# An mLSTM and feed-forward kernel on one core: raw query and key stacks, split on chip, and a result's round trip on GpSimd's queue

## The chip, the core and the metric

The kernel runs on one core of a Trainium2 chip. The core has five engines with a queue of instructions each: TensorE (PE) multiplies matrices, VectorE (DVE) and ScalarE (ACT) work on vectors, GpSimd (POOL) does the same more slowly, and SyncE (SP) issues DMA transfers. ACT and POOL can issue DMAs too. Every queue is worked off in order; an instruction that waits for a semaphore holds up everything behind it on its engine. Data lie in HBM, in the on-chip memory with 128 partitions (SBUF) and in the accumulators behind PE (PSUM). The metric is the device time of one execution in microseconds (us).

## The reference

For each of 4 x 8 chains (batch, head) a recurrent memory runs over 768 tokens, with head size 40; its output goes through a feed-forward layer of width 2048.

```python
def _attn_ref(q, k, v, i_gate, f_gate, o_gate):          # q, k, v: (4, 8, 768, 40)
    for t in range(S):
        m_new = np.maximum(f_gate[:, :, t] + m, i_gate[:, :, t])
        f_stab = np.exp(f_gate[:, :, t] + m - m_new)
        i_stab = np.exp(i_gate[:, :, t] - m_new)
        m = m_new
        C = f_stab[:, :, None, None] * C + i_stab[:, :, None, None] * np.einsum('bhd,bhe->bhde', vt, kt)
        n = f_stab[:, :, None] * n + i_stab[:, :, None] * kt
        h_tilde = np.einsum('bhde,bhe->bhd', C, qt)
        denom = np.maximum(np.abs(np.einsum('bhd,bhd->bh', n, qt)[:, :, None]), 1.0)
        y[:, :, t] = h_tilde / denom / (1.0 + np.exp(-o_gate[:, :, t]))

def _moe_ref(x, w_in, w_out):                            # x: (3072, 320)
    h = x @ w_in
    return (np.maximum(h, 0.0) + np.log1p(np.exp(-np.abs(h)))) @ w_out
```

## The kernel before

**Tiles and steps.** The 3072 tokens are cut into 24 steps of 128 tokens (one batch, one chunk of 128), and three steps make one tile of 384 tokens for the feed-forward layer: 8 tiles of 3 steps. A step does the memory in chunk form: scores of keys with queries (`scores`, PE tile sp), decays by a scan (`decay`, pw from fb), the product with the old state (`inter_wide`, iq), the values (`values_wide`, yq), and the new state (`state`, cp; cn). The first six steps (tiles 0 and 1) are "plain" and the other 18 "wide".

**The feed-forward layer.** For each of 16 chunks f of the hidden width, `products` multiplies the tile's input X with w_in into hp (8 matmuls), ACT takes the softplus twice (`activation`: gh rounded, and hp in place), DVE takes the difference gl, and two chunks later PE does 9 matmuls into po. Every number stands as a rounded high part and a remainder, since a single pass of PE keeps fewer bits. A tile's first matmul needs X of all three of its steps.

**Stacks of three.** A wide step's sp and iq use 120 partitions: three groups of 40, which hold q as (high, high, low) and k as (high, low, high), so that one pass sums the three partial products. Before the change `prepare` loads q and k of a whole tile (120 partitions are the three steps' 40 each), ACT rounds them (hiq, hik), POOL takes the remainders in place (loq, lok), and `load` copies six pieces of 40 partitions a step into the stacks qst and kst by DMA. The old state's stack cs is made otherwise (`stack`): ACT multiplies the threefold state with a mask of rows, lowk, and rounds; POOL subtracts that from the state. On masked rows the remainder is left, on the others the rounded value.

**The round trip of a step's result.** A wide step's result has the heads in pairs on partitions; `values_wide` writes y to HBM (yd, two DMAs), and `read_wide` reads it back by features (yx, three DMAs) and the denominators spread (nw, one). All six are issued from ACT's queue. Then `finish_wide` and `end_wide` make X: nm, its reciprocal and a product with the output gate eg on DVE, the product with yx on DVE, a rounding on ACT (X) and a subtraction on DVE.

**Order.** All instructions are put in order by a list of due times: one tick is one matmul of `products`. Each step has a base tick, and the numbers W_... are offsets to it; `-1000 - n` means n ticks after the last part. So a queue's order follows from the numbers, and the scheduler keeps it (`in_order`). In the wide stages the steps are a third of a tile, some 91 ticks, apart.

```python
    (W_LOAD, W_FB, W_SCAN, W_CN, W_CS, W_VW, W_SP0, W_SP1, W_Y, W_CP, W_CD,
     W_IQ0, W_IQ1, W_VI, W_YQ, W_YD, W_RD, W_FIN) = (
        -48, -52, 4, 19, -6, 4, 6, 14, 17, 31, 47, 50, 62, 38, 68, 79, 107, 139,
    )
```

Of the kernel before, what the change touches and what calls it, by code (L numbers as in the profile page):

```python
# [16 lines left out]
L = 128  # L17
NG = 3
# [21 lines left out]
def mlstm_moe_kernel(  # L40
# [44 lines left out]
    )  # L85
    GB = 3
# [54 lines left out]
    def later_gates():  # L141

        w = S - L
        ig = p1.tile([NCHAIN, w], F32, tag="hiq", name="ig")
        fg = p1.tile([NCHAIN, w], F32, tag="hik", name="fg")
# [13 lines left out]
        d1 = p1.tile([NCHAIN, w], F32, tag="loq", name="d1")  # L159
# [86 lines left out]
    def weights_out(u):  # L246
# [19 lines left out]
    def prepare(t):  # L266

        yield 0
        parts[t] = []
        for nm, src in zip("qk", qk[t]):  # L270
            lo = p1.tile([D3, H, L], F32R, tag=f"lo{nm}", name=f"lo{nm}{t}")
            nc.sync.dma_start(lo.bitcast(F32), src)
            parts[t].append([lo])
        yield PRD
        for (lo,), nm in zip(parts[t], "qk"):
            hi = p1.tile([D3, H, L], F32R, tag=f"hi{nm}", name=f"hi{nm}{t}")
            nc.scalar.copy(hi, lo.bitcast(F32))
            parts[t]["qk".index(nm)] = hi, lo
            yield -1000 - 5
        for hi, lo in parts[t]:  # L280
            for h in range(0, H, 4):
                h2 = slice(h, h + 4)
                nc.gpsimd.tensor_tensor(lo[:, h2], lo[:, h2].bitcast(F32), hi[:, h2], op=ALU.subtract)
                yield -1000 - PSY

    PRD, PSY = 24, 10

    parts = {}
# [5 lines left out]
    park = dpool.tile([B, D, H, E2], F32, name="park")  # L294
# [95 lines left out]
    def decays(z):  # L390

        z.fbs = []
        h0 = z.b * H
        for i in range(2):
            if z.s < 2:
                fb = ps_h.tile([128, HG, L], F32, tag="hp", name=f"fb{z.n}_{i}")
                for j in range(HG):
                    h = h0 + i * HG + j
                    nc.tensor.matmul(
                        fb[:, j, :], ident[:, h : h + 1].broadcast_to([128, 128]), fg0, start=True, stop=True  # L400
                    )
            else:
                fb = p2.tile([128, HG, L], F32, tag="fb", name=f"fb{z.n}_{i}")
                nc.sync.dma_start(fb, fz_d[z.c, h0 + i * HG : h0 + (i + 1) * HG, :].partition_broadcast(128))
            z.fbs.append(fb)
# [136 lines left out]
    def values_wide(z):  # L542

        yq = ps_a.tile([PP + EP, HG, L], F32, tag="pa", name=f"yq{z.n}")
        for h in range(H):
            p, i = divmod(h, 2)
            e0, e1 = i * PP, PP + i * EP
            nc.tensor.matmul(  # L548
                yq[e0:e1, p, :], z.via[:, h * E : h * E + e1 - e0], z.pws[h // HG][:, h % HG, :], start=True, stop=True
# [8 lines left out]
        rows = z.yd.rearrange("(d p i) t -> i d p t", p=HG, i=2)  # L558
        for i in range(2):
            nc.scalar.dma_start(rows[i], z.y[i * PP : i * PP + EP])  # L560

    def read_wide(z):
        z.yx = stage.tile([128, 3, L], F32, tag="sg", bufs=3, name=f"yx{z.n}")
        nc.scalar.dma_start(z.yx[:, 0:2], z.yd[0:256].rearrange("(c p) t -> p c t", p=128))
        for i in range(2):
            nc.scalar.dma_start(z.yx[i * 64 : (i + 1) * 64, 2], z.yd[256:DM])
        z.nq = p1.tile([128, L], F32, tag="sig", name=f"nw{z.n}")
        nc.scalar.dma_start(z.nq, z.yd[DM : DM + H].partition_broadcast(128 // H))
# [34 lines left out]

    def first_tile():
# [39 lines left out]
        for z in zs:  # L644
            z.sig = og[:, z.g].rearrange("p (h d) -> p h d", d=D)
# [63 lines left out]
        for i in range(NG, NH):  # L709
            nc.sync.dma_start(sgp[i], og[:, i])  # L710
# [252 lines left out]
    with in_order():  # L963
# [59 lines left out]
```

## Time and profile before

| what | value |
|---|---|
| median of 3 runs | 542.46 us (539.95 to 544.23) |
| the profiled execution | 546.57 us |
| its span, first to last instruction | 544.8 us |
| mean granted TensorE clock | 0.931 |
| DMA moved | 80.63 MB, mean 148 GB/s |

The span is what the trace covers; the execution's time has 1.7 us around it. A line of instruction groups reads: line of the kernel, engine, operation, what it writes and reads, shapes, count, then busy us and mean ns of one, then idle time of the engine ahead of it and what ended that. In a timeline a row has its start, its length, the engine (a q behind it marks its queue, which issues a DMA), and in brackets the idle time ahead and its releaser. In the list of waits a row is: who waited, for whom, us in all, times, longest us. A row of one tile's instructions has shortest, median and longest in ns. PE's ends are modelled, and a DMA's row is the time of its issue, not of its landing.

The DMA engines by slice of a 40th of the span, in tenths of full use:

```profile
DMA  7746881755553764648563866476664763111001
```

### The profile page before, as it was taken

The page shows a single profiled execution, that of the slowest core. Times are in us where ns is not written, and L with a number is a line of the kernel's source. Part 1 is how long each engine was busy: PE and PEld are TensorE (multiplying, and loading weights), DVE is VectorE, ACT ScalarE, POOL GpSimd, SP SyncE. Part 2 cuts the span into 40 slices and gives each one's busy share as a digit, 9 for nine tenths or more (in the row PEclk, how much of TensorE's full clock was granted, in tenths as well). Part 3 has the DMA queues.
Part 4 walks back from the last instruction along what each step waited for, and adds up shares of the span by engine and source line. Part 5 has one row for each costly group of instructions (what it writes and reads, how often), then busy time and mean ns, then how long its engine had stood idle before and what let it go on. Part 6 is the DMA issues. An engine that isn't in the chain of part 4 may idle for free.

```text
span 544.8 us, 9179 instructions
## 1 busy us (share of the span) xinstructions
PE 484.1 (89%) x3368; PEld 458.1 (84%) x3368; DVE 328.3 (60%) x522; ACT 206.1 (38%) x409; POOL 178.2 (33%) x217
## 2 busy tenths in 40 slices
PE   7478779787989868999889989998899979999997
PEld 7467678677989858999889978997899979999997
DVE  7776976976747536754675647672675566544221
ACT  2427343336325233425243253434342443234332
POOL 4258787986506203232205203510223211100000
PEclk9859887886999987999989999999899979999999
DMA  7746881755553764648563866476664763111001
GB/s 199 218 147 191 237 232 55 214 173 164 159 158 108 204 184 129 169 130 223 170 177 98 207 195 188 109 201 186 168 169 126 198 186 102 34 36 37 1 1 36
DMA packets 65951, 80.63 MB, mean 148 GB/s; under 512 B 7842, under 2 KB 46930, under 8 KB 65906
## 3 DMA queue, kind: packets, MB, share of 16 engines
q1 hardware_dynamic: 44594, 67.85, 44.4%
q10 hardware_dynamic: 21312, 12.20, 8.2%
q8 instruction: 26, 0.43, 0.3%
q14 instruction: 19, 0.16, 0.1%
HBM read 52.41 MB, written 8.30 MB: 111 GB/s over the span
## 4 chain that ended last, share of the span: by engine, by line
PE 58%; DMA 18%; DVE 9%; ACT 5%; issue 4%; POOL 3%; SPq 1%; ACTq 1%; DVEq 0%; POOLq 0%
PE hp L928 25%; PE po L899 23%; DMA yd<-y 5%; PE sp L484 3%; DMA fb<-fz_d 2%; PE cp L461 2%; PE yq L548 2%; DMA yx<-yd 2%; DMA eg<-in_oT 2%; DMA qst<-hiq 2%; DVE pw L413 2%; PE yp L517 1%; PE iq L537 1%; DMA cn<-cn 1%; DMA kst<-in_qk 1%
## 5 line engine op out<-in xcount | busy, mean ns | idle before, releaser
L928 PE MATMUL hp<-X,wih 128*128 128x384 f32 x768 | 191.4, 355 | 15.1 <-ACT X L585 12.5
L928 PEld LDWEIGHTS hp<-X,wih 128*128 128x128 f32 x768 | 140.0, 198 | 19.4 <-ACT X L585 13.9
L805 ACT ACTIVATE gh<-hp 128x384 fp32r<-128x384 f32 x128 | 62.6, 489 | 217.0 <-PE hp L928 116.7
L810 DVE TENSOR_TENSOR gl<-hp,gh 128x384 fp32r<-128x384 f32 x112 | 61.9, 553 | 127.0 <-ACT hp L807 126.8
L899 PE MATMUL po<-wol,gh 128*128 128x320 f32 x384 | 84.0, 320 | 7.7 <-POOL wol L252 7.7
L899 PE MATMUL po<-woh,gh 128*128 128x320 f32 x384 | 85.4, 321 | 6.1 <-ACT gh L805 3.9
L899 PE MATMUL po<-woh,gl 128*128 128x320 f32 x384 | 85.9, 321 | 0.0
L301 POOL TENSOR_TENSOR cs<-cn,cs 120x336 fp32r<-120x336 f32 x15 | 20.5, 1366 | 175.8 <-ACT cs L300 147.4
L899 PEld LDWEIGHTS po<-woh,gh 128*128 128x128 f32 x384 | 67.4, 196 | 8.6 <-ACT gh L805 4.8
L899 PEld LDWEIGHTS po<-wol,gh 128*128 128x128 f32 x384 | 63.8, 194 | 9.6 <-POOL wol L252 8.4
L928 PE MATMUL hp<-X,wil 128*128 128x384 f32 x256 | 71.2, 356 | 0.0
L413 DVE TENSOR_TENSOR_SCAN pw<-fb,ident 128x512 f32<-128x512 f32 x48 | 64.4, 1383 | 9.3 <-DMA fb<-fz_d 7.7
L899 PEld LDWEIGHTS po<-woh,gl 128*128 128x128 f32 x384 | 64.2, 194 | 0.6 <-issue 0.4
L807 ACT ACTIVATE hp<-hp 128x384 f32<-128x384 f32 x112 | 54.6, 487 | 0.0
L928 PEld LDWEIGHTS hp<-X,wil 128*128 128x128 f32 x256 | 47.8, 198 | 1.2 <-issue 0.9
L540 DVE TENSOR_TENSOR y<-iq,y 41x512 f32<-41x512 f32 x36 | 24.5, 681 | 32.6 <-PE iq L537 32.4
L484 PEld LDWEIGHTS sp<-qst,kst 120*128 120x128 f32 (+2 forms) x240 | 34.8, 204 | 6.7 <-issue 3.1
L484 PE MATMUL sp<-qst,kst 120*128 120x128 f32 (+2 forms) x240 | 35.7, 284 | 4.9 <-DVE X L599 2.7
L486 DVE TENSOR_TENSOR pw<-sp,pw 128x512 f32<-128x512 f32 x48 | 32.0, 681 | 1.9 <-PE sp L484 1.8
L585 ACT CAST X<-eg 128x384 fp32r<-128x384 f32 x18 | 9.2, 514 | 54.1 <-DVE eg L583 54.1
L810 POOL TENSOR_TENSOR gl<-ab,gh 128x384 fp32r<-128x384 f32 x16 | 19.5, 1219 | 12.7 <-ACT ab L807 11.1
L548 PE MATMUL yq<-pw,vi 128*64 128x128 f32 (+1 forms) x288 | 19.6, 278 | 2.8 <-DVE y L540 2.8
(124 smaller groups left out, 543.1 us busy)
## 6 DMA issues: line engine op xcount, KB each, us to landing
fb<-fz_d SPq DMA_DIRECT2D x44, 256.0 KB
vt<-in_vko SPq DMA_DIRECT2D x23, 324.0 KB
qst<-hiq SPq DMA_DIRECT2D x36, 160.0 KB
kst<-hik SPq DMA_DIRECT2D x36, 160.0 KB
wo<-in_w_out SPq DMA_DIRECT2D x8, 640.0 KB
wr<-in_w_in SPq DMA_DIRECT2D x8, 512.0 KB
out<-ob ACTq DMA_DIRECT2D x24, 160.0 KB
eg<-in_oT SPq DMA_DIRECT2D x6, 576.0 KB
```

Source lines behind the costliest of these rows:

```text
L301: nc.gpsimd.tensor_tensor(z.cs, z.old, z.cs, op=ALU.subtract)
L413: nc.vector.tensor_tensor_scan(pw.rearrange(flat), fb.rearrange(flat), ident4.rearrange(flat), 0.0, ALU.mult, ALU.add)
L461: nc.tensor.matmul(z.cp[:, h, :], z.kt[:, h * D : (h + 1) * D], z.vw[:, h, :], start=True, stop=True)
L484: nc.tensor.matmul(sp[:, j, :], z.kst[:, h, :], z.qst[:, h, :], start=True, stop=True)
L486: nc.vector.tensor_tensor(z.pws[i], sp, z.pws[i], op=ALU.mult)
L540: nc.vector.tensor_tensor(y, iq, y, op=ALU.mult)
L548: nc.tensor.matmul(yq[e0:e1, p, :], z.via[:, h * E : h * E + e1 - e0], z.pws[h // HG][:, h % HG, :], start=True, stop=True)
L805: nc.scalar.activation(gh, hp, AF.Softplus)
L807: nc.scalar.activation(ab, hp, AF.Softplus)
L810: (nc.vector if t else nc.gpsimd).tensor_tensor(gl, ab, gh, op=ALU.subtract)
L899: nc.tensor.matmul(po[j], a[:, j * 128 : (j + 1) * 128], w[:, f, :], start=(f == 0 and left[j] == 2), stop=(last and left[j] == 0),)
L928: nc.tensor.matmul(hp, a, r, start=(i == 0), stop=(i == len(seq) - 1))
```

## The change

- **Raw stacks.** The host lays q and k out per step and three times over, as 120 partitions of both. `prepare` and its four tiles go. A wide step loads all 120 partitions by one DMA (`load_raw`, due at -80), and `split` makes the stack as `stack` does the state's: per q and k one multiplication with a mask on ACT (lowq is new: 1 on the last 40 rows), then four subtractions of half the heads on POOL. q and k share one tile, qk. raw has one buffer, qk two.
- **The round trip** (yd, yx, nw) is issued from POOL's queue. The heads are paired (0, 4), (1, 5) and so on instead of (0, 1), (2, 3), so that y's rows and the decays behind it (fc) are runs of 2 KB instead of 512 bytes.
- **Smaller parts.** The parked state is written threefold by one DMA and read by one. fb is one tile per step with two buffers, loaded ahead of vt. The output gates of the first six steps come by three DMAs instead of six, q and k of the first tile by one each step instead of two.

```diff
-    def prepare(t):
...
+    def load_raw(z):
+
+        z.raw = p1.tile([D3, 2, H, L], F32, tag="raw", name=f"raw{z.n}")
+        nc.sync.dma_start(z.raw, qk[z.s])
+
+    def split(z):
+
+        z.qk = p2.tile([D3, 2, H, L], F32R, tag="qk", name=f"qk{z.n}")
+        z.qst, z.kst = z.qk[:, 0], z.qk[:, 1]
+        for i, low in enumerate((lowq, lowk)):
+            nc.scalar.activation(z.qk[:, i], z.raw[:, i], AF.Copy, scale=low[:D3])
+            yield SPA
+        for h in range(0, H, HG):
+            h2 = slice(h, h + HG)
+            for i in range(2):
+                nc.gpsimd.tensor_tensor(z.qk[:, i, h2], z.raw[:, i, h2], z.qk[:, i, h2], op=ALU.subtract)
+                yield SPL
+
+    SPA, SPL = 5, 7
...
-            (qh, ql), (kh, kl) = parts[t]
-            z.qst = p2.tile([D3, H, L], F32R, tag="qst", name=f"qst{n}")
-            z.kst = p2.tile([D3, H, L], F32R, tag="kst", name=f"kst{n}")
-            for r, (a, e) in enumerate(((qh, kh), (qh, kl), (ql, kh))):
-                nc.sync.dma_start(z.qst[r * D : (r + 1) * D].bitcast(F32), a[gs].bitcast(F32))
-                nc.sync.dma_start(z.kst[r * D : (r + 1) * D].bitcast(F32), e[gs].bitcast(F32))
...
-                for r in range(3 if t >= PLAIN else 1):
-                    nc.sync.dma_start(z.old[r * D : (r + 1) * D], park[z.b])
+                m = 3 if t >= PLAIN else 1
+                nc.sync.dma_start(z.old[0 : m * D].rearrange("p h e -> p (h e)"), park[z.b, 0:m].rearrange("r d f -> (r d) f"))
...
-            h = 2 * p + i
+            h = HG * i + p
...
-        rows = z.yd.rearrange("(d p i) t -> i d p t", p=HG, i=2)
+        rows = z.yd.rearrange("(d i p) t -> i d p t", p=HG, i=2)
         for i in range(2):
-            nc.scalar.dma_start(rows[i], z.y[i * PP : i * PP + EP])
+            nc.gpsimd.dma_start(rows[i], z.y[i * PP : i * PP + EP])
...
-        nc.scalar.dma_start(z.yx[:, 0:2], z.yd[0:256].rearrange("(c p) t -> p c t", p=128))
+        nc.gpsimd.dma_start(z.yx[:, 0:2], z.yd[0:256].rearrange("(c p) t -> p c t", p=128))
         for i in range(2):
-            nc.scalar.dma_start(z.yx[i * 64 : (i + 1) * 64, 2], z.yd[256:DM])
+            nc.gpsimd.dma_start(z.yx[i * 64 : (i + 1) * 64, 2], z.yd[256:DM])
...
-        nc.scalar.dma_start(z.nq, z.yd[DM : DM + H].partition_broadcast(128 // H))
+        nc.gpsimd.dma_start(z.nq, z.yd[DM : DM + H].partition_broadcast(128 // H))
...
     def wide_step(z):
-        yield W_LOAD if z.g else -45
-        load(z)
+        yield W_RAW
+        load_raw(z)
         yield W_FB
         decays(z)
+        yield W_LOAD
+        load(z)
+        yield from rel(split(z))
...
-    qk = np.stack(steps).reshape(NT, NG, 2, H, L, D).transpose(0, 2, 1, 5, 3, 4)
+    qk = np.stack(steps).transpose(0, 4, 1, 2, 3)
+    qk = np.concatenate([qk] * 3, axis=1)
```

**What moves on ACT.** ACT's queue ahead of a tile start, in the stage that ends at 323.87 us (gh_11 to X; names end in the chunk or step number and a count). Before:

```order
L805 ACTIVATE gh_11_2523<-hp_11_2508 128x384
L807 ACTIVATE hp_11_2508<-hp_11_2508 128x384
L564 DMA yx_3_2528<-yd_3_2460 128x2x128
L566 DMA yx_3_2528<-yd_3_2460 64x128 x2
L568 DMA nw_3_2532<-yd_3_2460 128x1x128
L805 ACTIVATE gh_12_2568<-hp_12_2550 128x384
L807 ACTIVATE hp_12_2550<-hp_12_2550 128x384
L336 ACT_TABLE_LOAD
L337 ACTIVATE eg_2475<-eg_2475 128x1152
L338 ACT_TABLE_LOAD
L805 ACTIVATE gh_13_2612<-hp_13_2589 128x384
```

And now:

```order
L811 ACTIVATE gh_11_2469<-hp_11_2452 128x384
L813 ACTIVATE hp_11_2452<-hp_11_2452 128x384
L811 ACTIVATE gh_12_2514<-hp_12_2496 128x384
L813 ACTIVATE hp_12_2496<-hp_12_2496 128x384
L318 ACT_TABLE_LOAD
L319 ACTIVATE eg_2419<-eg_2419 128x1152
L320 ACT_TABLE_LOAD
L358 ACTIVATE qk_5_2544<-raw_5_2459,lowq 120x1024
L358 ACTIVATE qk_5_2544<-raw_5_2459,lowk 120x1024
L811 ACTIVATE gh_13_2552<-hp_13_2538 128x384
```

The reads of yd are gone from between gh_11 and gh_12, and the two casts of the next step's stack stand between the second table load and gh_13.

**What moves on POOL.** POOL's queue over one wide step, from vw of one step to cs of the next. Before, at a place where no remainders of a tile fall:

```order
L440 TENSOR_TENSOR vw_4_2497<-vt_4_2380,gw_4_2494 128x328
L449 MEMSET cn_4_2541 40x8
L452 TENSOR_TENSOR cn_4_2541<-cn_3_2315,flast 40x8x41
L422 MEMSET vi_4_2582 128x7
L425 TENSOR_TENSOR vi_4_2582<-vt_4_2380,gT 128x328
L301 TENSOR_TENSOR cs_5_2715<-cn_4_2541,cs_5_2715 120x336
```

And now:

```order
L437 TENSOR_TENSOR vw_4_2441<-vt_4_2316,gw_4_2438 128x328
L563 DMA yx_3_2474<-yd_3_2404 128x2x128
L565 DMA yx_3_2474<-yd_3_2404 64x128 x2
L567 DMA nw_3_2478<-yd_3_2404 128x1x128
L446 MEMSET cn_4_2487 40x8
L449 TENSOR_TENSOR cn_4_2487<-cn_3_2264,flast 40x8x41
L419 MEMSET vi_4_2528 128x7
L422 TENSOR_TENSOR vi_4_2528<-vt_4_2316,gT 128x328
L363 TENSOR_TENSOR qk_5_2544<-raw_5_2459,qk_5_2544 120x512 x4
L559 DMA yd_4_2630<-y_4_2484 48x512 x2
L283 TENSOR_TENSOR cs_5_2659<-cn_4_2487,cs_5_2659 120x336
```

The reads of the step before stand between vw and cn, and the four subtractions and the write of the next result between vi and cs.

More of the change, by code (lines that the diff above doesn't have):

```diff
@@ L85, in mlstm_moe_kernel @@
     )
+    lowq = cpool.tile([128, 1], F32, name="lowq")
+    nc.gpsimd.memset(lowq, 1.0)
+    nc.gpsimd.affine_select(
+        lowq, lowq, pattern=[[0, 1]], compare_op=ALU.is_ge, fill=0.0, base=-2 * D, channel_multiplier=1
+    )
     GB = 3
@@ L143, in later_gates @@
         w = S - L
-        ig = p1.tile([NCHAIN, w], F32, tag="hiq", name="ig")
-        fg = p1.tile([NCHAIN, w], F32, tag="hik", name="fg")
+        ig = p1.tile([NCHAIN, w], F32, tag="ig", name="ig")
+        fg = p1.tile([NCHAIN, w], F32, tag="fg", name="fg")
         nc.sync.dma_start(fg, gates[0, :, L:])
@@ L158, in later_gates @@
         yield GR[2]
-        d1 = p1.tile([NCHAIN, w], F32, tag="loq", name="d1")
+        d1 = p1.tile([NCHAIN, w], F32, tag="raw", name="d1")
         nc.gpsimd.memset(d1, 0.0)
@@ L264, in mlstm_moe_kernel @@
     OF = [0, 8]
-    def prepare(t):
[L268 to L288, printed above, removed]
     Xs = {}
@@ L293, in mlstm_moe_kernel @@
     sgp = dpool.tile([NH, 128, DM], F32, name="sgp")
-    park = dpool.tile([B, D, H, E2], F32, name="park")
+    park = dpool.tile([B, 3, D, H * E2], F32, name="park")
     def stack(z):
@@ L401, in decays @@
                     )
[L402 to L405, printed above, removed]
+                z.fbs.append(fb)
+        if z.s >= 2:
+            fb = p2.tile([128, H, L], F32, tag="fb", bufs=FB, name=f"fb{z.n}")
+            for i in range(0, H, HG):
+                nc.sync.dma_start(fb[:, i : i + HG], fz_d[z.c, h0 + i : h0 + i + HG].partition_broadcast(128))
+            z.fbs = [fb[:, 0:HG], fb[:, HG:H]]
+    FB = 2
     def decay(z):
@@ L475, in new_state @@
         else:
-            nc.sync.dma_start(park[z.b], cn[0:D])
+            one = cn[0:D].rearrange("p h e -> p (h e)")
+            nc.sync.dma_start(park[z.b].rearrange("r d f -> d r f"), one.unsqueeze(1).broadcast_to([D, 3, H * E2]))
         yield
@@ L544, in values_wide @@
         yq = ps_a.tile([PP + EP, HG, L], F32, tag="pa", name=f"yq{z.n}")
-        for h in range(H):
-            p, i = divmod(h, 2)
+        for k in range(H):
+            p, i = divmod(k, 2)
+            h = HG * i + p
             e0, e1 = i * PP, PP + i * EP
             nc.tensor.matmul(
-                yq[e0:e1, p, :], z.via[:, h * E : h * E + e1 - e0], z.pws[h // HG][:, h % HG, :], start=True, stop=True
+                yq[e0:e1, p, :], z.via[:, h * E : h * E + e1 - e0], z.pws[i][:, p, :], start=True, stop=True
             )
@@ L602, in new_x @@
         Xs[t] = p2.tile([128, 6, T], F32R, tag="X", name=f"X{t}")
+    room = p1.tile([128, 2, H, L], F32, tag="raw", name="room")
     def first_tile():
@@ L626, in output_gates @@
         def output_gates(i0, i1):
-            for i in range(i0, i1):
-                b, c = ORDER[i]
-                nc.sync.dma_start(og[:, i], vko[b, c * L : (c + 1) * L, H * E + DM :])
+            part = vko[:, :, H * E + DM :].rearrange("b (c p) f -> p b c f", p=L)
+            if i0 == 0:
+                nc.sync.dma_start(og[:, 0:3], part[:, 0:3, 0])
+            else:
+                nc.sync.dma_start(og[:, 3], part[:, 3, 0])
+                nc.sync.dma_start(og[:, 4:6], part[:, 0, 1:3])
             yield
@@ L708, in first_tile @@
             state_values(z)
-        for i in range(NG, NH):
-            nc.sync.dma_start(sgp[i], og[:, i])
+        nc.sync.dma_start(sgp[NG:NH].rearrange("i p f -> p i f"), og[:, NG:NH])
         return zs
@@ L1003 @@
     arrays = {
-        "qk": qk.reshape(NT, 2, D3, H, L),
+        "qk": qk,
         "vko": np.concatenate([tok(v1), tok(k), tok(o)], axis=-1),
```

25 lines of the change are left out of this document (10 added, 15 removed).

## Prediction

> **What bounds the kernel now.** I read the page first (busy shares), then the stages of the five tiles between the first and the last two, then the waits of all engines, then the timeline ahead of one tile start.
>
> ```profile
> span 544.8 us, 9179 instructions
> PE 484.1 (89%) x3368; PEld 458.1 (84%) x3368; DVE 328.3 (60%) x522; ACT 206.1 (38%) x409; POOL 178.2 (33%) x217
> ```
>
> TensorE (PE) is the bound: no other engine is busy for more than 60%. The profiled execution took 546.57 us, 1.7 more than its span. What a change of the attention part can win is therefore PE's idle time, and time in which PE runs at a lower clock. The stages, each from one tile's first product to the next tile's, show both (microseconds from start to end, length, then busy time of each engine, granted clock, DMA):
>
> ```profile
> 143.13:206.44 63.31, 52.76 (x386) 49.37 (x384) 35.95 (x59) 22.85 (x46) 15.80 (x19) 0.95 0.60 166
> 206.44:263.71 57.27, 56.09 (x416) 53.62 (x417) 35.86 (x61) 22.13 (x43) 15.35 (x22) 0.97 0.59 164
> 263.71:323.87 60.16, 55.83 (x401) 52.76 (x401) 36.16 (x61) 22.83 (x45) 14.69 (x19) 0.97 0.61 169
> 323.87:383.22 59.35, 54.02 (x401) 51.19 (x401) 35.49 (x61) 22.75 (x45) 13.87 (x19) 1.00 0.64 170
> 383.22:442.32 59.10, 56.15 (x416) 53.49 (x416) 36.74 (x63) 22.75 (x45) 15.32 (x22) 0.97 0.62 170
> sum 299.19, PE 274.86 PEld 260.43 DVE 180.22 ACT 113.31 POOL 75.02; mean PE 54.97 PEld 52.09 DVE 36.04 ACT 22.66 POOL 15.00
> ```
>
> In these 299.2 us PE is idle for 299.19 - 274.86 = 24.3. GpSimd (POOL, the fifth busy column) works 14 to 16 us of about 60 in a tile, so it has room. The fourth tile, at clock 1.00, is busy 54.02 us; the three with 0.97 are busy 56.09, 55.83 and 56.15, together 6.0 us more, for about the same work. Who PE waited for, and what stood in the way on ACT:
>
> ```profile
> ACT gh L805 <- DMA yx<-yd: 36.0, 8, 7.2
> ACT gh L805 <- DMA yd<-y: 17.3, 4, 9.0
> PE hp L928 <- ACT X L585: 12.5, 5, 3.1
> PE po L899 <- POOL wol L252: 7.7, 3, 3.4
> PE po L899 <- ACT gh L805: 3.9, 2, 3.7
> PE cp L461 <- POOL cn L449: 2.9, 2, 1.6
> PE yq L548 <- DVE y L540: 2.8, 2, 1.8
> PE po L899 <- ACT ob L948: 1.9, 1, 1.9
> ```
>
> Five tile starts wait for X, 12.5 us in all. The other waits in the same stages come to 3.9 + 2.9 + 2.8 + 1.9 = 11.5, and 12.5 + 11.5 = 24.0 is nearly all of the 24.3. The wait for wol is in tile 0. ACT itself sat 36.0 + 17.3 us behind the write and reads of yd. One tile start shows how the two belong together:
>
> ```profile
> 301.76 0.64 ACTq L560 DMA_DIRECT2D yd<-y  x1
> 304.49 0.56 ACTq L560 DMA_DIRECT2D yd<-y  x1
> 306.83 0.91 POOL L301 TENSOR_TENSOR cs<-cn,cs 120x336 fp32r<-120x336 f32 x1 [11.23 <-DVE pw L413]
> 310.94 0.38 ACTq L564 DMA_DIRECT2D yx<-yd  x1
> 313.21 0.62 ACTq L568 DMA_DIRECT2D nw<-yd  x1
> 313.93 0.49 ACT L805 ACTIVATE gh<-hp 128x384 fp32r<-128x384 f32 x1 [6.42 <-DMA yx<-yd]
> 314.82 1.28 ACT L336 ACT_TABLE_LOAD   x1
> 318.60 0.49 ACT L805 ACTIVATE gh<-hp 128x384 fp32r<-128x384 f32 x1
> 319.50 0.56 DVE L810 TENSOR_TENSOR gl<-hp,gh 128x384 fp32r<-128x384 f32 x1 [3.52 <-ACT hp L807]
> 320.81 0.29 DVE L572 SCALAR_TENSOR_TENSOR nm<-nw 128x128 f32<-128x128 f32 x1
> 323.30 0.51 ACT L585 CAST X<-eg 128x384 fp32r<-128x384 f32 x1 [3.04 <-DVE eg L583]
> 323.87 1.21 PE L928 MATMUL hp<-X,wih 128*128 128x384 f32 x5 [2.45 <-ACT X L585]
> ```
>
> ACT's queue is in order. The read yx has to wait until the write of yd has landed (304.49 to 310.94), and gh, which needs only PE, stands behind it: ACT is idle for 6.42 us. The sigmoid with its two table loads (314.82 to 318.60) then comes late, the next gh with it, DVE's gl waits for that (3.52), and behind gl in DVE's queue stands nm, the first step to X. X comes 2.45 us late. POOL idled 11.23 us in that same stretch.
>
> **The change, part by part.** First the write and reads of yd, six DMAs a step, which go from ACT's queue to POOL's. What they and the work added cost:
>
> ```profile
> L283 POOL TENSOR_TENSOR loq<-loq,hiq x12: 1269/1287/2242, 78.2 to 409.0; 120x512 fp32r<-120x512 f32 x12
> L277 ACT CAST hiq<-loq x6: 1043/1050/1055, 72.1 to 403.1; 120x1024 fp32r<-120x1024 f32 x6
> L301 POOL TENSOR_TENSOR cs<-cn,cs x15: 907/954/1917, 116.6 to 465.7; 120x336 fp32r<-120x336 f32 x15
> L425 POOL TENSOR_TENSOR vi<-vt,gT 128x328 f32<-128x328 f32 x23 | 18.0, 784 | 5.3 <-DMA vt<-in_vko 5.3
> L440 POOL TENSOR_TENSOR vw<-vt,gw 128x328 f32<-128x328 f32 x19 | 14.6, 768 | 15.0 <-DVE gw L434 7.8 <-PE hp L928 3.0 <-PE sp L484 1.7
> L452 POOL TENSOR_TENSOR cn<-cn,flast 40x328 f32<-40x328 f32 x13 | 11.8, 904 | 0.0
> L560 ACTq DMA_DIRECT2D yd<-y x36: 565/611/1497, 141.0 to 479.8; - x36
> L566 ACTq DMA_DIRECT2D yx<-yd x36: 482/607/1453, 148.9 to 484.3; - x36
> L564 ACTq DMA_DIRECT2D yx<-yd x18: 366/383/429, 148.5 to 483.3; - x18
> L568 ACTq DMA_DIRECT2D nw<-yd x18: 548/606/911, 150.2 to 485.0; - x18
> ```
>
> *ACT's side.* At the tile start shown ACT loses its 6.42 us wait, and gains the two casts of the next step, 2 x 1.05 = 2.1 us, behind the table loads and ahead of gh_13. Net 6.42 - 2.1 = 4.3 us earlier, against 2.45 that X was late and 3.1 at the worst. So the five waits for X should nearly go. I leave 0.5 us each: 12.5 - 2.5 = 10.0 won. The waits for gh (3.9) and ob (1.9) are ACT's own and go: 5.8. Those of yq for DVE y (2.8) come from gl ahead of y in DVE's queue; I count 2.0. The wait for cn (2.9) I leave, since POOL's DMAs now stand ahead of cn.
>
> *POOL's side.* No DMA of POOL stands in this trace. The nearest rows are the same DMAs on ACT: at the medians 2 x 0.611 + 0.383 + 2 x 0.607 + 0.606 = 3.4 us a step, at the longest 2 x 1.497 + 0.429 + 2 x 1.453 + 0.911 = 7.2. At the shortest they are 3.0; a price below that, or a gain on POOL, is excluded because POOL had no DMA to lose. I take 6.0, or 1.0 each, nearer to the long end, because POOL does like work slower than the others. The Trainium skill (DMA: Bandwidth & Descriptors, section Latency and other measured facts) gives a DMA from GpSimd about 1 us to its first byte and one from SP or ACT about 0.6. By that page the six would be about 6 us as well; no run here shows it.
>
> A step's other work on POOL: four splits 4 x 1.287 = 5.1 (per step, before it was per tile), cs 0.95, vw 0.77, vi 0.78, cn 0.90, together 8.5. With the DMAs 14.5, between 11.5 and 15.7. A step has a third of a tile, 59.35 / 3 = 19.8 us, or 18.8 when 3 us of waiting a tile are gone. It fits, with 4.3 to spare. Behind POOL's wait for the landing of yd stand cn, vi and the splits of the next step. Cn is then about 4 x 1.0 us later than before; DVE's addition to cn would wait 1 to 2 us, and gl behind it has a lead of about two chunks on PE. For these new waits on PE (sp for qk, cp for cn) I put +1.5, from 0 to 5.
>
> *Raw stacks, one load.* Per step SP issues one DMA of 120 x 8 KB = 983 KB from HBM in place of six copies of 164 KB within the chip (983 KB as well) and a third of two loads of 492 KB. That is 328 KB and about six issues less. It is hidden beside PE either way; if it is not, the cast on ACT waits for it (a rival below). The load of fb moves ahead of that of vt in SP's queue; that costs nothing while vt lands before vi and vw, which come after the scan of fb. If vt came late, POOL would wait at vw, and yx behind it. The casts grow from two per tile to six, 4 x 1.05 = 4.2 us of ACT's 22.7 busy in a tile: hidden, and already counted at the tile start.
>
> *Clock.* The three stages at 0.97 were busy 6.0 us longer than the one at 1.00 would have been; if the lower clock comes from PE's idle time, it goes with it. The trace does not tie the two together, so I count half, 3.0 (0 to 6.0). The Trainium skill (TensorE: Matmul & The Clock Gate, Part 1) has the clock drop after an idle window of about 3.4 us; by that page waits of 3.1 us are too short, the term would be 0 and the sum -14.3.
>
> *Tile 0.* POOL is nearly full there. The splits of the first two wide steps cost 8 x 1.287 = 10.3 where four (5.1) stood before; the four of the first step come later than the old ones did, ahead of wol. POOL's idle time stands at the end of tile 0:
>
> ```profile
> 131.65 1.01 POOL L810 TENSOR_TENSOR gl<-ab,gh 128x384 fp32r<-128x384 f32 x1 [3.92 <-ACT ab L807]
> 141.21 1.71 POOL L252 TENSOR_TENSOR wol<-sgo,woh 128x320 fp32r<-128x320 f32 x2 [1.52 <-ACT woh L249]
> ```
>
> There 3.92 + 1.52 us cover the second step's four; PE's wait for wol (7.7) grows by the rest. I put +2.5, between 0 and 5.1.
>
> *First loads.* Q, k and og of the first tile come by fewer issues; the DMA engines were full there, so -0.5 (from +1, as both memsets now precede the load, to -2). Park (one threefold write and one load in place of three), fb's second buffer and the new pairing of heads add nothing to PE, DVE or ACT; SP's queue, which computes nothing, covers them, and were it late, the scan would wait for fb.
>
> **Sum.** -10.0 - 5.8 - 2.0 + 1.5 - 3.0 + 2.5 - 0.5 = -17.3 us. Against the profiled execution's 546.57 that is 529.3. The median of the runs shown is 542.46, 4.1 below that execution, and the change is compared by medians: 542.46 - 17.3 = 525.2, rounded 525.
>
> **Rivals.** (1) *X stays late.* The write of yd now stands behind four splits on POOL, and yx behind vw. For it: yx still waits for a landing, which took 5.9 us (305.05 to 310.94) in the stretch shown. Against it: cs ran there at 306.83 and vw takes 0.77 behind it, so both were done well ahead of yx at 310.94. The terms for X and clock then fall away: -17.3 + 13.0 = -4.3, or 538.
>
> (2) *POOL becomes the bound*, which ends slower. POOL's step is 8.5 + 6d against 18.8, so it decides from d = 1.7 us on. At d = 2.0 a step needs 20.5, 1.7 more, and over some 17 intervals +29: 542.5 - 17.3 + 29 = 554. For it: POOL's own rows stretch beside DVE, 1.287 to 2.242. Against it: that is the longest of twelve, and even ACT's longest issues make 1.2 on average. The Trainium skill (SBUF — State Buffer, section SBUF: two separate sides) warns of such a case: GpSimd cannot write its descriptors while VectorE is in a two-port mode. By that page VectorE's copies within SBUF do this, and the wide steps have none of these; no run here shows it.
>
> (3) *The load of raw lands late.* There is one buffer, so it starts only when the last split has read it, some 6 us ahead of the cast. If the cast on ACT waits 3 us at each tile start, X is late again by about as much: -17.3 + 15 = -2, or 540.
>
> **Chances.** The forecast 0.70, rival 1 0.13, rival 2 0.12, rival 3 0.05. A measurement of this kernel tells 1% (5.4 us) from no change: faster is below 537.0, slower above 547.9. The forecast's case is faster, 0.70. Rivals 1 and 3 lie within 1%, but with a longer wait rival 3 ends slower, for which I take 0.02 of its 0.05: same 0.13 + 0.03 = 0.16, slower 0.12 + 0.02 = 0.14. The low end of the range takes all 24.3 us of idle time, 6.0 of clock and 2 of first loads, less 2.5 for tile 0: -29.8, or 513. The high end takes in rivals 1 and 3: 541. That leaves out rival 2 and the tails.
>
> **What would show it.** Right: ACT's waits for yd and yx are gone; PE's wait for X is under 3 us in all; the stages are 55 to 57 us long; POOL is busy (with its queue) 40 to 47 us a tile. Rival 1: PE waits for X behind POOL's yx. Rival 2: sp waits for qk, cp for cn, in every step. Rival 3: ACT's cast waits for raw. The forecast fails if POOL's DMAs take over 1.8 us each, or if tile 0 loses more than 5 us.

## The result, and the profile after

| | before | changed |
|---|---|---|
| median of 4 runs | 543.35 us (539.95 to 545.69) | 559.49 us (556.51 to 562.45) |
| ratio | 1 | 1.0302 (95% interval 1.0223 to 1.0381) |
| the profiled execution | 546.57 us | 556.51 us |
| its span | 544.8 us | 554.8 us |
| mean granted TensorE clock | 0.931 | 0.941 |

The changed kernel is 3% slower; the forecast was 525 us, 3% faster. The profiled execution of the kernel before lies above its four runs, that of the changed kernel is the fastest of its four, so their spans differ by 10.0 us where the medians differ by 16.

Section 1 of the page of the changed kernel gives each engine's busy time:

```profile
PE 483.8 (87%) x3368; PEld 455.5 (82%) x3368; DVE 377.0 (68%) x522; ACT 232.4 (42%) x433; POOL 299.5 (54%) x375
```

PE is as busy as before (484.1), so what was lost is waiting. DVE is 48.7 us busier (328.3 before) with the same 522 instructions: some of them have become longer. The tables of instruction groups say which, first one row of before, then rows of the changed kernel:

```profile
L572 DVE SCALAR_TENSOR_TENSOR nm<-nw 128x128 f32<-128x128 f32 x18 | 5.2, 288 | 0.3
...
L571 DVE SCALAR_TENSOR_TENSOR nm<-nw 128x128 f32<-128x128 f32 x18 | 51.6, 2865 | 2.9 <-DMA nw<-yd 2.7
L363 POOL TENSOR_TENSOR qk<-raw,qk 120x512 fp32r<-120x512 f32 x72 | 93.8, 1327 | 1.6 <-ACT qk L358 1.5
L563 POOL DMA_DIRECT2D yx<-yd x18 | 14.1, 782 | 65.7 <-DMA yd<-y 65.7
L559 POOL DMA_DIRECT2D yd<-y x36 | 19.4, 540 | 54.9 <-DVE y L552 54.9
L565 POOL DMA_DIRECT2D yx<-yd x36 | 18.9, 529 | 0.0
L567 POOL DMA_DIRECT2D nw<-yd x18 | 10.0, 554 | 0.0
```

The 18 nm took 5.2 us before (0.29 each) and take 51.6 now. That is 46.4 of the 48.7 us. The list of PE's waits has, beside those of the first tiles, these:

```profile
PE hp L934 <- ACT X L584: 10.0, 5, 3.0
PE cp L458 <- POOL vw L437: 7.6, 6, 1.5
PE iq L535 <- DVE cn L463: 5.9, 7, 1.5
PE yq L547 <- POOL vi L422: 5.4, 3, 2.5
```

X is nearly as late as before (12.5), and PE now waits for vw, cn and vi, all of which are POOL's or behind POOL. It never waits for the subtractions themselves: no wait of sp for POOL's qk is in the list. The timeline ahead of the tile start at 328.53, the one that answers to 323.87 before, shows why:

```profile
308.64 1.07 POOL L559 DMA_DIRECT2D yd<-y  x2 [3.37 <-DVE y L552]
310.27 1.06 POOL L283 TENSOR_TENSOR cs<-cn,cs 120x336 fp32r<-120x336 f32 x1 [0.56 <-ACT cs L282]
312.75 0.74 POOL L437 TENSOR_TENSOR vw<-vt,gw 128x328 f32<-128x328 f32 x1 [1.41 <-PE hp L934]
316.64 0.79 POOL L563 DMA_DIRECT2D yx<-yd  x1 [3.16 <-DMA yd<-y]
318.48 0.55 POOL L567 DMA_DIRECT2D nw<-yd  x1
319.83 0.75 POOL L422 TENSOR_TENSOR vi<-vt,gT 128x328 f32<-128x328 f32 x1
320.52 5.08 POOL L363 TENSOR_TENSOR qk<-raw,qk 120x512 fp32r<-120x512 f32 x4
322.65 3.11 DVE L571 SCALAR_TENSOR_TENSOR nm<-nw 128x128 f32<-128x128 f32 x1
325.79 0.95 DVE L572 RECIPROCAL nm<-nm 128x128 f32<-128x128 f32 x1
327.37 0.56 DVE L582 TENSOR_TENSOR eg<-yx,eg 128x384 f32<-128x384 f32 x1
327.85 0.68 DVE L552 TENSOR_TENSOR y<-yq,y 112x512 f32<-112x512 f32 x1
327.96 0.51 ACT L584 CAST X<-eg 128x384 fp32r<-128x384 f32 x1 [5.61 <-DVE eg L582]
328.98 1.07 POOL L559 DMA_DIRECT2D yd<-y  x2 [3.37 <-DVE y L552]
```

Two things can be read here. First, nm starts in the midst of POOL's four subtractions and ends 0.16 us after the last of them (325.60). Secondly, the rows close a loop. The next step's y stands behind nm in DVE's queue, and its write yd, issued at 328.98, stands behind the subtractions in POOL's. From yd to yd it is 8.0 us to the reads (issue and landing), 2.4 of reads, 1.5 of cn and vi, 5.1 of subtractions, 0.2 until nm has ended, and 3.2 over the reciprocal, the gate, the product and y to the next yd: 20.34 us. Three steps make 61.0 us, and the last three wide stages took 60.6, 61.7 and 62.7 us (from the tile starts at 267.92, 328.53, 390.21 and 452.88). The chain that ended last says the same: from 149 to 454 us it goes back and forth between the landing of yd and nm, but for stretches of PE of 11 to 14 us behind the tile starts at 208.51, 267.92 and 328.53.

```profile
309.20 6.69 DMA yd<-y
322.65 3.12 DVE nm L571
...
350.36 6.33 DMA yd<-y
363.52 3.04 DVE nm L571
...
391.23 6.99 DMA yd<-y
404.50 3.55 DVE nm L571
```

### The profile page after: what moved, and what is told of

Its sections match the earlier page's. It is cut to its first block, busy times and chain, and to the rows that moved or that the text cites. A ratio compares the mean times of both kernels' runs of the same rounds, so it can differ in the third digit from the quotient of the medians.

```text
span 554.8 us, 9099 instructions
## 1 busy us (share of the span) xinstructions
PE 483.8 (87%) x3368; PEld 455.5 (82%) x3368; DVE 377.0 (68%) x522; ACT 232.4 (42%) x433; POOL 299.5 (54%) x375
## 4 chain that ended last, share of the span: by engine, by line
PE 28%; DVE 25%; DMA 20%; POOL 14%; issue 9%; ACT 3%; SPq 1%; POOLq 0%; DVEq 0%; ACTq 0%
DMA yd<-y 16%; PE hp L934 12%; PE po L905 11%; DVE nm L571 8%; DVE y L538 2%; DVE nm L572 2%; POOL qk L363 2%; DVE gl L816 2%; POOL yx L563 2%; DVE pw L410 2%; DMA ig<-in_gates 2%; POOL cn L449 2%; DVE eg L574 1%; DVE eg L582 1%; DVE y L552 1%
## 5 line engine op out<-in xcount | busy, mean ns | idle before, releaser
L934 PE MATMUL hp<-X,wih 128*128 128x384 f32 x768 | 189.1, 351 | 13.0 <-ACT X L584 10.0
L363 POOL TENSOR_TENSOR qk<-raw,qk 120x512 fp32r<-120x512 f32 x72 | 93.8, 1327 | 1.6 <-ACT qk L358 1.5
L905 PE MATMUL po<-woh,gh 128*128 128x320 f32 x384 | 83.4, 317 | 0.0
L410 DVE TENSOR_TENSOR_SCAN pw<-fb,ident 128x512 f32<-128x512 f32 x48 | 72.6, 1553 | 1.3 <-PE fb L392 1.3
L813 ACT ACTIVATE hp<-hp 128x384 f32<-128x384 f32 x112 | 54.4, 486 | 0.0
L571 DVE SCALAR_TENSOR_TENSOR nm<-nw 128x128 f32<-128x128 f32 x18 | 51.6, 2865 | 2.9 <-DMA nw<-yd 2.7
L563 POOL DMA_DIRECT2D yx<-yd x18 | 14.1, 782 | 65.7 <-DMA yd<-y 65.7
L463 DVE TENSOR_TENSOR cn<-cn,cp 40x328 f32<-40x328 f32 x16 | 7.8, 488 | 61.0 <-POOL cn L449 56.4
L559 POOL DMA_DIRECT2D yd<-y x36 | 19.4, 540 | 54.9 <-DVE y L552 54.9
L482 PEld LDWEIGHTS sp<-qk 120*128 120x128 f32 (+2 forms) x224 | 34.1, 213 | 9.2 <-issue 4.2
L482 PE MATMUL sp<-qk 120*128 120x128 f32 (+2 forms) x224 | 35.4, 294 | 6.6 <-DVE X L598 2.8
```

Of the source, the lines that this page charges most:

```text
L363: nc.gpsimd.tensor_tensor(z.qk[:, i, h2], z.raw[:, i, h2], z.qk[:, i, h2], op=ALU.subtract)
L410: nc.vector.tensor_tensor_scan(pw.rearrange(flat), fb.rearrange(flat), ident4.rearrange(flat), 0.0, ALU.mult, ALU.add)
L482: nc.tensor.matmul(sp[:, j, :], z.kst[:, h, :], z.qst[:, h, :], start=True, stop=True)
L559: nc.gpsimd.dma_start(rows[i], z.y[i * PP : i * PP + EP])
L563: nc.gpsimd.dma_start(z.yx[:, 0:2], z.yd[0:256].rearrange("(c p) t -> p c t", p=128))
L571: nc.vector.scalar_tensor_tensor(nm, z.nq, -1.0, z.nq, op0=ALU.mult, op1=ALU.max)
```

## The experiments

Two theories were set against others. **Lock**: an instruction of DVE with both operands in SBUF, such as nm, is held up for as long as POOL runs subtractions. **Loop**: the closed chain above sets the pace, so that each microsecond on it costs some 17 us in all, until PE is the bound again. Their first rival was **queue**: POOL's wait for the landing of yd holds the kernel up, whatever else is done. Each ratio is to runs of the kernel before taken along with that kernel, whose medians were 541.76 to 544.48 us.

| kernel | median us | ratio to before (95% interval) | nm, mean us | PE's wait for X, us |
|---|---|---|---|---|
| changed | 559.49 | 1.0302 (1.0223 to 1.0381) | 2.87 | 10.0 |
| DMAs on POOL alone | 538.56 | 0.9927 (0.9892 to 0.9961) | 0.34 | 3.7 |
| raw stacks alone | 569.94 | 1.0478 (1.0398 to 1.0557) | 0.79 | 19.5 |
| reciprocal first | 545.54 | 1.0050 (1.0010 to 1.0090) | 1.97 (absolute value) | 6.5 |
| y ahead of nm | 542.62 | 0.9975 (0.9935 to 1.0015) | 0.68 | 11.2 |
| half the subtractions behind yd | 551.51 | 1.0129 (1.0072 to 1.0186) | 0.36 | 2.9 |
| all four ahead of the reads | 588.94 | 1.0843 (1.0777 to 1.0909) | 0.32 | 7.9 |
| two ahead, two behind the reads | 580.85 | 1.0745 (1.0665 to 1.0825) | 0.61 | 9.1 |
| no subtractions | 517.21 | 0.9506 (0.9446 to 0.9566) | 0.29 | 1.9 |
| fills in place of subtractions | 531.85 | 0.9810 (0.9727 to 0.9892) | 0.29 | 0.8 |
| subtractions on DVE | 528.41 | 0.9748 (0.9681 to 0.9816) | 0.29 | 2.7 |

**The two halves of the change.** The kernel before with the six DMAs issued by POOL:

```diff
-            nc.scalar.dma_start(rows[i], z.y[i * PP : i * PP + EP])
+            nc.gpsimd.dma_start(rows[i], z.y[i * PP : i * PP + EP])
```

(and so for yx and nw).

> The kernel before with nothing changed but the queue of the write and reads of yd, which GpSimd issues. Theory lock: few subtractions beside nm, so nm stays under 0.8 us in the mean, PE's wait for X falls from 12.5 us to under 5, time 525 to 536, as was predicted for the queue's part. Theory queue: GpSimd's wait for the landing makes cn, vw and cs late, PE's waits for these are over 10 us, time 548 or more.

The median is 0.7% below the kernel before. PE's wait for X fell from 12.5 to 3.7 us, as predicted for this part; nm stayed short; but PE now waits 7.8 us for vw, and the time lies 2.6 us above the expected range. The queue alone is a small gain, far from the rival's 548 or more, so the rival falls. The other half, the changed kernel with these DMAs on ACT:

```diff
-            nc.gpsimd.dma_start(rows[i], z.y[i * PP : i * PP + EP])
+            nc.scalar.dma_start(rows[i], z.y[i * PP : i * PP + EP])
```

> The changed kernel with the write and reads of yd back on ScalarE's queue; the raw stacks and their subtractions on GpSimd stay. Theory lock: the subtractions still run when nm does, nm's mean stays over 1.2 us, ScalarE's waits for yd (over 40 us in all) come back on top, time 545 to 560, not faster than the kernel before. Theory queue: without its waits GpSimd is early, time at or below 542.

Neither theory had this: 570 us, slower than both, and nm at 0.79 us in the mean. ACT waits 72.8 us for yd at gh, the casts stand behind that wait, and POOL waits 124.8 us for the casts. X is late by another path. The raw stacks are what costs: +4.8% with ACT's queue, and from 0.9927 to 1.0302 with POOL's.

**Which instruction waits.** DVE's two instructions on nw change places:

```diff
-        nc.vector.scalar_tensor_tensor(nm, z.nq, -1.0, z.nq, op0=ALU.mult, op1=ALU.max)
-        nc.vector.reciprocal(nm, nm)
+        nc.vector.reciprocal(nm, z.nq)
+        nc.vector.scalar_tensor_tensor(nm, nm, -1.0, nm, op0=ALU.mult, op1=ALU.max)
```

> The changed kernel with two instructions of VectorE swapped: the reciprocal (one operand in SBUF) runs first on nw, and the absolute value (two operands) on its result. Theory lock: the reciprocal keeps its 0.95 us beside the subtractions, the absolute value takes the wait, 1.5 to 2.5 us in the mean; the loop is 0.95 us a step shorter, stages 58 to 59.5 us, time 542 to 550. Rival, that the first reader of nw waits for the data: the reciprocal takes about 3.5 us, the absolute value 0.29, and the time stays within 1% of 559.

One tile's instructions, with shortest, median and longest in ns:

```profile
L571 DVE RECIPROCAL nm<-nw x18: 942/952/954, 166.1 to 491.7; 128x128 f32<-128x128 f32 x18
L572 DVE SCALAR_TENSOR_TENSOR nm<-nm x18: 291/2107/3276, 167.0 to 492.6; 128x128 f32<-128x128 f32 x18
```

The reciprocal reads nw first and is never longer than 0.95 us, though 16 of the 18 ran beside subtractions; the absolute value, with two operands, is held up. So it is not the data that are late. The loop became 0.9 us shorter, and the median fell by 14 us, as 0.95 us over some 15 steps would give; the two profiled spans, 554.8 and 547.3 us, differ by only 7.5.

**Cutting the loop.** One number puts the next y ahead of nm on DVE:

```diff
-    AWAY = 18
+    AWAY = 27
```

> The changed kernel with one number changed (AWAY 27 for 18): on VectorE's queue the next step's y stands ahead of nm instead of behind the four instructions from nm to the product with yx. Theory loop (the pace is set by the closed chain yd, landing 6.7 us, reads, cn, vi, subtractions, nm, y, next yd, 20.3 us a step): the chain from nm to the next yd is cut, so stages fall from 61 to 56 to 59 us although nm stays blocked for 2 to 3 us, time 532 to 547. Rival, X alone (each blocked nm costs only what X is late at a tile start): X is another 0.7 us later, stages as long as before, time 556 to 566.

The time fell by 17 us to that of the kernel before. The stages between the same tile starts are 59.7, 56.9, 56.3 and 57.9 us, from 59.4, 60.6, 61.7 and 62.7. The wait for X stayed (11.2 us): X was not what set the pace. That nm would stay blocked was wrong; with another phase between the engines it mostly met no subtractions, and 12 of the 18 took 0.28 us. So this run alone does not tell the loop from the lock.

**Moving the subtractions.** The second two of each step go behind the write of yd:

```diff
         for h in range(0, H, HG):
             h2 = slice(h, h + HG)
+            if h:
+                yield SPH
...
-    SPA, SPL = 5, 7
+    SPA, SPL, SPH = 5, 7, 13
```

> The changed kernel with the subtractions of the second four heads moved on GpSimd's queue behind the write of yd, where GpSimd then waits for the landing anyway; those of the first four stay behind vi, casts and load stay. Theory loop: 2.5 us of subtractions leave the chain, nm is blocked under 1 us, the chain is 17.5 to 18 us a step and PE sets the pace, stages 56 to 58 us, time 527 to 540. Rival: what GpSimd does in a step costs the same wherever it stands, cs and vw come later instead, time 552 or more.

Only 8 us were won: the time lies 11.5 us above the expected range, just under the rival's 552. nm is free, but the two scans of the next step now stand beside the moved subtractions and cs. Timeline rows of this kernel:

```profile
305.61 5.92 DVE L412 TENSOR_TENSOR_SCAN pw<-fb,ident 128x512 f32<-128x512 f32 x2
305.91 2.56 POOL L365 TENSOR_TENSOR qk<-raw,qk 120x512 fp32r<-120x512 f32 x2
...
308.44 0.90 POOL L283 TENSOR_TENSOR cs<-cn,cs 120x336 fp32r<-120x336 f32 x1
```

Two scans take 2.4 us undisturbed; here they take 3.5 more, which is the length of the three instructions of POOL (2.56 + 0.90). The lock has found the next instruction with two operands in SBUF. PE also waits 13.6 us for qk, and ACT 11.8 us for raw. Two other orders put subtractions ahead of the reads, first all four, then two:

```diff
-        yield W_LOAD
-        load(z)
+        yield W_SPLIT
         yield from rel(split(z))
+        yield W_FB
+        decays(z)
+        yield W_LOAD
+        load(z)
...
-    SPA, SPL = 5, 7
+    SPA, SPL = 5, 1
+    W_SPLIT = -95
```

> The changed kernel with the four subtractions of a step's stack moved on GpSimd's queue from behind vi to ahead of the reads of yd (and the load of raw 47 ticks earlier), so that they fill GpSimd's wait for the landing of yd and no longer run when nm does. Theory lock (nm, an instruction with two operands in SBUF, is blocked on VectorE for as long as GpSimd subtracts, and so the loop from one step's yd over the reads, the subtractions and nm to the next step's yd takes 20.3 us instead of some 17): nm's mean falls from 2.87 us to under 0.7, PE's wait for X from 10 us to under 3, stages from 61 to 56 to 57.5 us, time 525 to 538. Theory queue (GpSimd's wait for the landing of yd is what holds the kernel, wherever the subtractions stand): nm's mean falls too, but the reads are late behind the subtractions instead, stages stay over 60, time 552 or more.

```diff
...
+        if z.s > 8:
+            yield -93
+            yield from rel(split(z))
...
-            ev += [(W_CN, lambda: old_state(z)), (W_VW, lambda: last_decays(z)), (W_VW, lambda: state_values(z))]
+            ev += [(5, lambda: old_state(z)), (W_VW, lambda: last_decays(z)), (W_VW, lambda: state_values(z))]
...
-        ev += [(W_VI, lambda: gate_values(z)),
+        ev += [(6, lambda: gate_values(z)),
```

> The changed kernel with another order on GpSimd's queue in the wide steps from the fourth on: yd, cs, vw, cn, two subtractions, vi, reads, two subtractions; raw is loaded 70 ticks earlier. The first two then lie in the wait for the landing of yd, after the scans have ended, and the last two run while nw is under way. Theory loop and lock: neither the scans nor nm stand beside subtractions for more than 0.6 us, the chain from yd to yd is 16 to 17 us, PE sets the pace, nm under 0.8 us and a scan under 1.6 us in the mean, stages 56 to 58 us, time 524 to 540. Rival, as in the run with all four ahead of the reads: the load of raw into its one buffer lands late, ScalarE's casts wait for it over 20 us in all, time 552 or more.

Both are misses, and the slowest of all, although nm is nearly free in them (0.32 and 0.61 us). In both ACT waits for raw, 38.0 us in the first kernel and 45.2 in the second, and cs and vw stand behind the casts. Rows of the first kernel, from one load of raw to the next:

```profile
318.75 0.45 SPq L351 DMA_DIRECT2D raw<-in_qk  x1
326.54 1.15 ACT L358 ACTIVATE qk<-raw,lowq 120x1024 fp32r<-120x1024 f32 x1 [3.50 <-DMA raw<-in_qk]
331.63 5.08 POOL L363 TENSOR_TENSOR qk<-raw,qk 120x512 fp32r<-120x512 f32 x4
339.09 0.77 POOL L450 TENSOR_TENSOR cn<-cn,flast 40x328 f32<-40x328 f32 x1
339.89 0.49 DVE L464 TENSOR_TENSOR cn<-cn,cp 40x328 f32<-40x328 f32 x1 [8.56 <-POOL cn L450]
340.44 0.75 SPq L470 DMA_DIRECT2D cn<-cn  x1
342.06 0.45 SPq L351 DMA_DIRECT2D raw<-in_qk  x1
```

Here raw is read out at 336.71, but its next load stands in SP's queue behind the copies of cn, and cn comes on POOL behind the subtractions and the reads (SP waits 236.7 us for cn, PE 21.3 us at iq). So another loop has closed, of 23.3 us a step; three make 70, and the stages are 66 to 69 us long. In the second kernel it is the one buffer: raw is loaded only when the last subtraction of the step before has read it, and SP waits 167.7 us for that. The first run's rival had named the time, but not this cause, so the run does not tell the two theories apart; the second run's rival had named both the time and the late raw. In the changed kernel ACT waits for raw once, 1.9 us.

**What the subtractions cost in all, and how.** First they are left out (the remainders are then missing from the result):

```diff
-        for h in range(0, H, HG):
-            h2 = slice(h, h + HG)
-            for i in range(2):
-                nc.gpsimd.tensor_tensor(z.qk[:, i, h2], z.raw[:, i, h2], z.qk[:, i, h2], op=ALU.subtract)
-                yield SPL
```

> The changed kernel without the four subtractions on GpSimd, so that the stacks hold only the rounded values and zeros (the remainders are left out of the result); load and casts stay. Theory loop: all that the raw stacks cost is these 5.1 us a step on GpSimd, the chain is 15 us, PE sets the pace, nm takes 0.29 us, time 522 to 535. Rival, that the load of 983 KB a step, the casts on ScalarE or the first tiles cost as much: time 542 or more, with waits for raw or for the casts.

The time is 517.21 us, 42 below the changed kernel and 5 below the expected range, and stages are 53.5 to 54.4 us long but for the first (58.6). So all the rest of the change, with its load of 983 KB a step and its casts, is a gain of 5%. Then POOL is kept busy as long at the same places, by fills that write SBUF and read nothing:

```diff
-                nc.gpsimd.tensor_tensor(z.qk[:, i, h2], z.raw[:, i, h2], z.qk[:, i, h2], op=ALU.subtract)
+                nc.gpsimd.memset(z.raw.rearrange("p i h t -> p (i h t)")[:, 0:1440], 0.0)
```

> The changed kernel with each of the four subtractions of a step replaced by a fill of 120x1440 elements of the same place's raw buffer, at some 1.2 to 1.3 us each, so that GpSimd is busy as long and at the same points of its queue but reads nothing from SBUF (the remainders are left out of the result). Theory lock: a fill does not hold up nm, which takes 0.29 us; the chain from yd to yd is 2.8 us shorter, 17.5 us, PE sets the pace, time 516 to 530, near the run without subtractions. Rival, that the 5.1 us of GpSimd's in-order time are what costs, whatever it does in them: time 545 or more, with nm short and yd waiting behind the fills; or nm is held up by fills as by subtractions, 2 us or more in the mean.

Again single tiles, with shortest, median and longest in ns:

```profile
L363 POOL MEMSET raw<- x72: 1291/1302/1522, 100.6 to 446.0; 120x1440 f32 x72
L571 DVE SCALAR_TENSOR_TENSOR nm<-nw x18: 280/292/295, 165.2 to 474.3; 128x128 f32<-128x128 f32 x18
```

A fill is as long as a subtraction (1.31 us in the mean against 1.33), and 16 of the 18 nm ran beside one, as 16 ran beside subtractions in the changed kernel; but no nm waits for a fill. The time is 2 us above the expected range. So of the 42 us, 559.49 - 531.85 = 27.6 are the lock, and 531.85 - 517.21 = 14.6 are POOL's own time (by the ratios to the kernel before about 27 and 17), of which 8.7 have been lost by the end of the first wide stage (207.08 us against 198.41), where POOL is still busy with the weights.

**A version that leaves nothing out.** DVE subtracts:

```diff
-                nc.gpsimd.tensor_tensor(z.qk[:, i, h2], z.raw[:, i, h2], z.qk[:, i, h2], op=ALU.subtract)
+                nc.vector.tensor_tensor(z.qk[:, i, h2], z.raw[:, i, h2], z.qk[:, i, h2], op=ALU.subtract)
```

> The changed kernel with the four subtractions of a step on VectorE instead of GpSimd, at the same due times. Theory lock: nothing of GpSimd's blocks nm any more (0.29 us), GpSimd's part of the chain is 5.1 us shorter; VectorE is busy some 4 x 0.68 = 2.7 us a step more and 2.6 less for nm, so the time comes near the run without subtractions: 518 to 532. Rival, that VectorE's queue becomes the bound, since gl and y stand behind the subtractions and these behind ScalarE's casts: PE waits for gl or y over 15 us in all, time 542 or more.

Instruction groups of DVE in this kernel:

```profile
L363 DVE TENSOR_TENSOR qk<-raw,qk 120x512 fp32r<-120x512 f32 x72 | 50.2, 709 | 4.5 <-ACT qk L358 4.5
...
L571 DVE SCALAR_TENSOR_TENSOR nm<-nw 128x128 f32<-128x128 f32 x18 | 5.2, 288 | 1.3 <-DMA nw<-yd 1.0
```

It takes 528.41 us and beats both kernels: 2.5% below the kernel before, 5.5% below the changed one. DVE needs 50.2 us for the subtractions and no longer loses 46.4 at nm. The rival does not occur: PE waits 2.3 us for y and never for gl. The stages are 55.7 to 57.2 us but for the first (60.0), which is what the prediction had wanted of the change.

## Why the prediction was wrong

**The step that failed** is the one on POOL's side: the subtractions were costed by busy time alone ("It fits, with 4.3 to spare"), with 1.5 us for new waits and 2.5 in tile 0. Measured, they cost 42 us. POOL did have room: behind the first wide stage it was busy 34 to 35 us in stages of 59 to 63 us, less than the 40 to 47 foreseen. What it was checked for was whether POOL keeps up. Two other questions were not asked: what on DVE cannot run while POOL does (27.6 us), and whether the chain through POOL's and DVE's in-order queues closes on itself, so that such a wait delays every step behind it. With the chain cut, 17 us came back, in part because nm then met fewer subtractions.

The trace of the kernel before had the first answer. Of DVE's scans and gw, both with two operands in SBUF, the shortest, median and longest ns were there:

```profile
L413 DVE TENSOR_TENSOR_SCAN pw<-fb,ident x48: 1186/1215/2244, 6.8 to 464.2; 128x512 f32<-128x512 f32 x48
L434 DVE TENSOR_TENSOR gw<-gT,pw x40: 128/159/893, 9.0 to 448.7; 128x4 f32<-128x4 f32 x40
```

Of the scans beside which no tensor instruction of POOL ran, none took over 1.23 us; all the longer ones stood beside one. The prediction looked at POOL's rows that stretch beside DVE (1.287 to 2.242), and not at DVE's that stretch beside POOL. What it cited on GpSimd and VectorE was about a DMA's descriptors. The Trainium skill (SBUF — State Buffer, section Who interferes with whom) says that an instruction of VectorE with two operands in SBUF and one of GpSimd that reads SBUF shut each other out, that one which only writes does not, and that one operand in SBUF is no conflict. The traces agree in each of the three: 2.87 us for nm beside subtractions, 0.29 beside fills, 0.95 for the reciprocal beside subtractions.

Neither of the two signs by which the prediction said that it would fail came: no DMA of POOL took over 0.80 us, and tile 0 did not become longer.

**The waits for X, 10.0 won.** The cause was read rightly: ACT's waits for yd are gone, and with the queue moved alone X's wait fell to 3.7. In the change 2.5 were won, since nm is part of the way to X.

**gh and ob, 5.8.** Right: neither stands among PE's waits now. **yq, 2.0.** The wait for DVE's y is gone, another for POOL's vi (5.4 in three times) came.

**New waits, +1.5 (0 to 5).** Mis-sized: vw 7.6 and cn 5.9, from 2.9 before for cn.

**POOL's DMAs, 6.0 a step.** Too dear: 2 x 0.540 + 0.782 + 2 x 0.529 + 0.554 = 3.5 us, as ACT's 3.4. The Trainium skill's figure of about 1 us (DMA: Bandwidth & Descriptors, section Latency and other measured facts) is a time to the first byte; the queue was held for 0.53 to 0.78 us an issue.

**Clock, -3.0.** Did not come in the change, where PE's waits stayed: 0.941 from 0.931, with PE as busy as before. Where the waits went, it came. The last four of the five stages without subtractions, and a stretch of the changed kernel behind a wait of 1.86 us for X at 328.53 (length, then busy time of each engine, clock, DMA):

```profile
198.41:252.81 54.40, 54.40 (x416) 51.94 (x416) 35.61 (x61) 26.62 (x48) 20.36 (x34) 1.00 0.61 162
252.81:306.29 53.48, 53.48 (x402) 51.25 (x401) 36.50 (x61) 27.33 (x50) 19.25 (x33) 1.00 0.68 169
306.29:360.70 54.41, 53.59 (x402) 51.29 (x401) 35.49 (x60) 27.39 (x50) 18.98 (x33) 1.00 0.65 170
360.70:415.11 54.41, 54.41 (x417) 51.94 (x417) 36.73 (x63) 27.44 (x50) 20.48 (x36) 1.00 0.62 166
...
329.36:332.77 3.41, 3.41 (x14) 3.41 (x14) 3.41 (x4) 1.25 (x3) 1.59 (x3) 0.50 0.98 202
```

In those four stages PE is busy for 215.9 us, against 56.09 + 55.83 + 54.02 + 56.15 = 222.1 before, 6.2 us less, which is the whole of the term's range; the kernel's mean of 0.947 is low because of the stages ahead (0.82 in tile 0). In the changed kernel the clock was halved for 3.41 us four times between 141 and 453 us, each time behind a wait of PE of 1.86 to 3.00 us; others, of 1.84 us (266.08) and 3.35 us (143.23), left it at 1.00. So the traces do tie the clock to PE's waits, though not to every one, and the prediction was right to expect that the lower clock would go with them. The Trainium skill's idle window of about 3.4 us (TensorE: Matmul & The Clock Gate, Part 1), by which the term would have been 0, does not fit: shorter waits were enough.

**Tile 0, +2.5, and first loads, -0.5.** The other way round: tile 0's first product came 1.45 us later (37.05 to 38.50), and tile 0 was 0.6 us shorter (103.31 to 102.74), though PE's wait for wol grew from 7.7 to 8.7. The DMA engines were not full there, but busy for 70% of the first 37 us. The next stage became 1.2 longer (66.08 to 67.27). The prediction's list starts that stage at 143.13; its first product is at 140.36.

**The rivals.** The outcome lies on the side of rival 2, but not by its mechanism, which needed 1.7 us a DMA. Rival 3, a late raw, did not occur in the change (1.9 us, once), and did in the two orders with subtractions ahead of the reads. Rival 1 had X late behind POOL; X was late, but behind nm.

## What to carry to other kernels

Before work is put on an idle GpSimd, look at which of VectorE's instructions with two operands in SBUF will run beside it, and at the longest of their rows in the trace; an engine that has room by its busy time can still shut out another. Follow what is moved through the in-order queues until it comes back to itself: where such a chain of writes, landings and waits takes longer than the step, it is the bound, though every engine has idle time. Where the conflict can't be scheduled away, the same work on VectorE (0.71 us in the mean, against 1.33 on GpSimd) may be the cheaper.

## What was not expected of the hardware

The lock is mostly not handed over between instructions of GpSimd that follow each other directly. nm, started at 322.65 in the second of four subtractions, ran only when the fourth had ended; in another step it took 4.29 us, over the end of vi and three of them. So it went in 15 of the 16 steps in which nm met subtractions; in the other (223.50, 0.44 us) it ran between the third and the fourth. With half of them behind yd, the first scan was held over two subtractions and cs in nine steps and took 4.8 us at the longest; but in five steps the second scan ran between the two subtractions, and the later of these took 2.2 us instead of 1.3. What decides between the two, these traces do not show. Moving two of the four elsewhere only changed the victim, from nm to the scans.
